# Attention steps of a fused decay-attention and two-MLP kernel: y, scores and decayed operands placed in three units instead of two

## Chip, cores and metric

One core of one Trainium2 chip. The metric is device time in microseconds (us), the median of the runs shown. Engines: TensorE (PE, with its weight loads as PEld), VectorE (DVE), ScalarE (ACT), GpSimd (POOL), SyncE (SP, which here only issues DMAs).

## What is computed

A decayed linear attention over r, k, v (4 x 8 heads x 768 tokens x 48), followed by two MLPs on 3072 tokens of width 384 with 2048 hidden columns. Cut to its core:

```python
for t in range(S):                       # attention, state [B, H, D, D]
    cur = einsum('bhd,bhe->bhde', u * k_t, v_t)
    y[:, :, t] = einsum('bhd,bhde->bhe', r_t, state + cur)
    state = w * state + einsum('bhd,bhe->bhde', k_t, v_t)
x = y.transpose(0, 2, 1, 3).reshape(B * S, H * D)
h = x @ w_in;  x = maximum(h, 0) ** 2 @ w_out          # layer 1
h = x @ w_in2; out = (h - tanh(h)) @ w_out2            # layer 2
```

## The kernel before

**Blocks and units.** The 3072 tokens are six blocks (`j`) of 512. A layer of a block is 16 units (`f`), one for each 128 hidden columns. A unit has `gemm1` (L579: 9 matmuls of 128x512 into `h`) and `gemm2` (L619 in layer 1, L729 in layer 2: 9 matmuls into the three banks `acc`). Each float32 operand is held as a high and a low part, so that a product is three matmuls of parts; `hi` and `lo` of the hidden values are `ghi` and `glo`. The loop over `units` runs all of layer 1 and then all of layer 2. In each turn it issues `gemm1` and the activation of a later unit (`front`, one unit ahead in most of block 0, two ahead after) and then `gemm2` of its own.

**Attention steps.** 24 steps of 128 tokens (two sub-steps of 64) make up the six blocks. Steps 0 to 3 are computed before the loop. Steps 4 to 23 are spread over the units of layer 1, four in each of blocks 0 to 4, where block j computes the steps of block j+1. A step i has these parts:

- `load` (L188 to L196): five DMAs on SP's queue for r/k (`rkt`), r (`rnt`), k (`kn`) and v (`vs`).
- `att_u`, `att_r`, `att_k`, `att_d` (L276 to L308) on POOL and the reduction `att_s` (`bt`, L293) on VectorE. They go through the list `nat_q`: `nat_push` puts six entries in, `nat_pop` issues two in each unit.
- `att_a` (L319, two of L322): k and r times the decay tables, on VectorE, into `rkt` and `ra`. `state_0` (L382 on ScalarE, L385 on VectorE): copies of the state into `vs`, and the decayed state.
- `att_b` (L351, 32 matmuls): scores `sc`. `att_v` (L362, 32 matmuls): state products `pv`.
- `att_m` (L372, two on VectorE): the masked scores into `ra`. `state_1` (L399, L385, L404 on VectorE, two L382 on ScalarE): the new state.
- `att_c` (L413, 32 matmuls): y from `ra` and `vs`. `att_e`: two copies on ScalarE (`ys`, `xt`, L430) and two subtractions on VectorE (L432). `pack` (L440): six DMAs.

Scores, state and y have one PSUM bank each (5, 6, 7). `vs` has three buffers, `ra`, `kn`, `rkt` and `rnt` have two.

**Weights of layer 1.** All 16 units' weights are converted while block 0 runs and stay on the chip. For unit f: `load_w` (L70, SP, three buffers `raw`), `conv0` (L84, ScalarE), `conv1` (L92 and L93, VectorE), `conv2` (L101, ScalarE: the high part), `conv3` (L107, the low part; on VectorE in the loop, on POOL before it). In turn f of block 0 the kernel issues `conv2` and `conv3` of unit f+2, `load_w` of f+5, `conv1` of f+3 and, at the end, `conv0` of f+4. `act1_low` (L608, VectorE) makes `glo` in blocks 0 and 5; in blocks 1 to 4 POOL does (L599). Layer 2's weights are converted in the same way from block 4 on: in its unit 11 the attention's memory is given back, the constants of layer 2 are set and five `load_w` are issued; `conv0(2, 0)` comes in unit 12.

**Order.** The schedule is manual: every engine and queue works through its instructions in the order in which the program issues them, and only waits between engines shift them. In a turn of block 0 the order before is: `glo` of the unit, conv2 and conv3, `load_w`, `front`, conv1, then the attention parts, `gemm2`, `att_m` and `state_1`, the two of `nat_pop`, conv0. In units 1, 4, 7, 10 (`visit`) the attention parts are `att_b(i+1)`, `att_v(i+1)`, `att_c(i)`, `att_e(i)`, `pack(i)`, `load(i+3)`; in units 0, 3, 6, 9 they are `att_a` and `state_0` of the step whose scores follow in the next unit.

Of the kernel before, what the change touches and what calls it, by code (L numbers as in the profile page):

```python
# [25 lines left out]
def decay_attention_moe_moe_kernel(  # L26
# [11 lines left out]
    NTAU, GP, _, NP, C = rk.shape  # L38
# [7 lines left out]
    NB = NT // TB  # L46
    TPB = TB // C
# [33 lines left out]
    def conv0(layer, f):  # L81
        if f < NF:
            lo, hi = words(layer, f)
            nc.scalar.activation(  # L84
                out=hi.bitcast(F32), in_=hi.bitcast(F32), func=AF.Prelu,
                scale=2.0 ** -112, alpha=2.0 ** 32,
            )
# [203 lines left out]
    def att_s(i):  # L291
        bt_t[i] = a2.tile([128, 2, NP], F32, tag="bt", name="bt")
        nc.vector.tensor_reduce(  # L293
            out=bt_t[i].rearrange("p c P -> p (c P)"), in_=rn_t[i].rearrange("p (x d) -> p x d", d=D),
            axis=mybir.AxisListType.X, op=ALU.add,
        )
# [445 lines left out]
        del acc[j]  # L742


    visit = {1: 0, 4: 1, 7: 2, 10: 3}
    units = [(1, j, f) for j in range(NB) for f in range(NF)]
    units += [(2, j, f) for j in range(NB) for f in range(NF)]

# [16 lines left out]
    with tc.manual_schedule():  # L765
        table_a()
        clear()
        for i in range(TPB):
            first(i)
            if i == 2:  # L770
                load_w(1, 0)
        for a in range(2):
            nc.scalar.dma_start(out=ub[half(a)], in_=u[1:2, a * GPS:(a + 1) * GPS].to_broadcast([64, GPS]))
        load_w(1, 1)
        load_w(1, 2)
        setup_pool()
        fill(WARM)
        V, G = nc.vector, nc.gpsimd

        def rs(i):  # L780
            if i != 3:
                lead_r(i, V)
            lead_s(i)

        def mb(i):
            for e in range(2):
                lead_m(2 * i + e)
                if i + 1 < TPB:
                    lead_b(2 * i + 2 + e)

        lead_z(0)
        lead_z(1)
        table_b()
        lead_a(0)
        lead_u(0, G)
        lead_zc(0)
        lead_b(0)
        lead_b(1)
        rs(0)
        lead_d(0)  # L800
        lead_zc(1)
        table_c()
        table_d()
        lead_u(1, G)
        lead_a(1)
        lead_k(0, G)
        fill(FILL[0])
        mb(0)
        lead_u(2, G)
        rs(1)  # L810
        lead_d(1)
        lead_k(1, G)
        lead_a(2)
        for i in range(TPB):
            lead_c(i)
            fill(FILL[1][i])
            if i + 2 < TPB:
                rs(i + 2)
            if i + 1 < TPB:
                mb(i + 1)  # L820
            if i < 2:
                load(i + 4)
            lead_e(i)
            if i + 2 < TPB:
                lead_zc(i + 2)
                lead_d(i + 2)
                lead_k(i + 2, G)
            if i + 3 <= TPB:
                (lead_u if i + 3 < TPB else att_u)(i + 3, G)
            if i + 3 < TPB:  # L830
                if i == 0:
                    lead_r(3, G)
                lead_a(i + 3, G)
            if i == 0:
                conv0(1, 0)
                conv1(1, 0)
                conv2(1, 0)
                conv3(1, 0, G)
            if i == 1:
                conv0(1, 1)  # L840
                att_r(4, G)
            if i == 2:
                conv1(1, 1)
            if i == 3:
                conv2(1, 1)
                conv3(1, 1, G)
        load_w(1, 3)
        conv0(1, 2)
        att_s(4)
        att_d(4, 0)  # L850
        att_d(4, 1)
        front(0)
        att_a(4)
        state_0(4)
        att_k(4, G)
        att_b(4)
        att_v(4)
        conv1(1, 2)
        att_m(4)
        state_1(4)  # L860
        nat_push(5)
        load_w(1, 4)
        load(6)
        conv2(1, 2)
        conv3(1, 2, G)
        load_w(1, 5)
        conv0(1, 3)
        nat_pop(3)
        front(1)
        nat_pop(3)  # L870

        nf = 2
        for n, (layer, j, f) in enumerate(units):
            if layer == 1:
                act1_low(j, f)
            if layer == 1 and j == 0 and f:
                conv2(1, f + 2)
                conv3(1, f + 2, V)
                if f + 5 < NF:
                    load_w(1, f + 5)  # L880
            if layer == 1 and j == NB - 1 and 0 < f < NF - 1:
                conv2(2, f - 1)
                conv3(2, f - 1, V)
            while nf < len(units) and nf <= n + look(n):
                front(nf)
                nf += 1
            att = layer == 1 and j + 1 < NB and f in visit
            if layer == 1 and j == 0:
                conv1(1, f + 3)
            if layer == 1 and j + 1 < NB and f - 2 in (-2, 1, 4, 7):  # L890
                i = TPB * (j + 1) + visit.get(f - 2, -1) + 2
                if i < NTAU:
                    att_a(i)
                    state_0(i)
            if att:
                i = TPB * (j + 1) + visit[f]
                if i + 1 < NTAU:
                    att_b(i + 1)
                    att_v(i + 1)
                att_c(i)  # L900
                att_e(i)
                pack(i)
                load(i + 3)
            if layer == 2 and j == 0 and f in (1, 2):
                conv2(2, NF - 3 + f)
                conv3(2, NF - 3 + f, G)
            if layer == 1:
                gemm2_1(j, f)
            else:
                gemm2_2(j, f)  # L910
            if att and i + 1 < NTAU:
                att_m(i + 1)
                state_1(i + 1)
                nat_push(i + 2)
            if layer == 1:
                nat_pop()
            if layer == 1 and j == 0:
                conv0(1, f + 4)
            if layer == 1 and j == NB - 2:
                if f == 11:  # L920
                    at_ctx.close()
                    open2()
                    for q in range(5):
                        load_w(2, q)
                if f == 12:
                    conv0(2, 0)
                if f == 14:
                    conv1(2, 0)
                    conv0(2, 1)
            if f == NF - 1:  # L930
                (evac1 if layer == 1 else evac2)(j)
            if layer == 1 and j == NB - 1:
                conv1(2, f + 1)
                conv0(2, f + 2)
                prep_x2(0, f)
            if layer == 2 and j + 1 < NB:
                prep_x2(j + 1, f)
# [72 lines left out]
```

## Time and profile before

| | |
|---|---|
| median of 3 runs | 943.94 us (943.58 to 943.96) |
| profiled execution | 943.92 us |
| its span, first to last instruction | 942.1 us |
| mean granted TensorE clock | 0.976 |
| busy: PE, DVE, ACT, POOL | 898.2, 650.8, 632.9, 251.1 us |

A profile is one execution. "Busy" is the time in which an engine had an instruction running. In rows of a timeline, the start and the length of a group of instructions come first, both in us; a bracket at the end is the idle time of that engine just before it and what ended it. "x9" is the number of instructions. The granted clock (PEclk) is 1.00 at 2.4 GHz and 0.50 at 1.2 GHz. Times in us from the start of the span.

### The profile page before, as it was taken

To read this page: it belongs to the slowest core of one execution; us is meant where nothing else is said; L and a number is where in the kernel's file an instruction comes from. 1 tells how busy PE (TensorE), PEld (TensorE's weight loads), DVE (VectorE), ACT (ScalarE), POOL (GpSimd) and SP (SyncE) were. 2 spreads that over 40 slices of the span, in tenths; PEclk is the share of its full clock that TensorE was granted. 3 is DMA by queue.
4 is the path that set the end of the run, shared out by engine and by line. 5 is a ranking of instruction groups with operands and counts; after the bars stand their busy time and mean duration, and the time that the engine had idled before them with its cause. 6 is when DMAs were issued, how large, how long until landed. Compare 5 with 4: busy or idle time off the path is not lost.

```text
span 942.1 us, 14863 instructions
## 1 busy us (share of the span) xinstructions
PE 898.2 (95%) x5688; PEld 739.4 (78%) x5688; DVE 650.8 (69%) x1016; ACT 632.9 (67%) x1121; POOL 251.1 (27%) x214
## 2 busy tenths in 40 slices
PE   6778889999999999999999999999999999999997
PEld 5656667888788788878888877888888888888885
DVE  8868886351424153133157789999999999999997
ACT  2535556444454545444478888898898988988985
POOL 4753332555365356444301011001001001000000
PEclk7978899999999999999999999999999999999999
DMA  8824442232132123120346210010010100100000
GB/s 241 236 85 151 151 152 67 62 90 59 49 84 77 57 56 93 49 84 9 130 167 213 98 57 12 1 56 12 1 57 13 56 12 1 56 12 0 34 1 34
DMA packets 32167, 67.72 MB, mean 72 GB/s; under 512 B 5600, under 2 KB 17888, under 8 KB 32096
## 3 DMA queue, kind: packets, MB, share of 16 engines
q1 hardware_dynamic: 31792, 66.48, 22.6%
q8 instruction: 45, 0.74, 0.3%
q10 hardware_dynamic: 304, 0.30, 0.1%
q14 instruction: 26, 0.21, 0.1%
HBM read 55.35 MB, written 9.44 MB: 69 GB/s over the span
## 4 chain that ended last, share of the span: by engine, by line
PE 80%; DVE 10%; ACT 4%; DMA 2%; POOL 2%; issue 1%; ACTq 0%; DVEq 0%; POOLq 0%
PE h L579 36%; PE o L729 19%; PE acc L619 17%; PE y L413 3%; PE sc L351 2%; PE pv L362 2%; DVE raw L93 1%; DVE ra L322 1%; DVE w L107 1%; DVE raw L92 1%; DMA x2d<-x2s 1%; DMA first_kv<-in_nat_dram 1%; DVE rkt L319 1%; DMA vtab<-in_w_dram 1%; DVE ra L372 1%
## 5 line engine op out<-in xcount | busy, mean ns | idle before, releaser
L579 PE MATMUL h<-xt,w 128*128 128x512 f32 x864 | 213.2, 392 | 0.0
L579 PE MATMUL h<-xs,w 128*128 128x512 f32 x864 | 211.5, 389 | 0.0
L579 PEld LDWEIGHTS h<-xt,w 128*128 128x128 f32 x864 | 163.2, 189 | 34.4
L579 PEld LDWEIGHTS h<-xs,w 128*128 128x128 f32 x864 | 162.2, 188 | 34.1
L619 PE MATMUL acc<-ghi,w 128*128 128x512 f32 x576 | 152.9, 396 | 3.5 <-ACT x2s L635 3.5
L729 PE MATMUL o<-ghi,w 128*128 128x512 f32 x576 | 148.9, 390 | 0.3 <-ACT ghi L700 0.3
L619 PEld LDWEIGHTS acc<-ghi,w 128*128 128x128 f32 x576 | 106.9, 189 | 28.0 <-ACT x2s L635 5.2
L599 POOL TENSOR_TENSOR glo<-g,ghi 128x512 fp32r<-128x512 f32 x64 | 84.0, 1313 | 164.3 <-PE acc L619 96.8
L593 ACT ACTIVATE g<-h 128x512 f32<-128x512 f32 x96 | 57.3, 597 | 104.3 <-PE h L579 104.1
L729 PEld LDWEIGHTS o<-ghi,w 128*128 128x128 f32 x576 | 107.7, 188 | 24.1 <-ACT ob L740 1.3
L432 DVE TENSOR_TENSOR ys<-y,ys 112x128 fp32r<-112x128 f32 x20 | 5.8, 292 | 149.9 <-ACT xt L430 149.9
L652 POOL TENSOR_TENSOR xs<-x2f,xs 128x512 fp32r<-128x512 f32 x18 | 24.4, 1354 | 316.7 <-DVE xs L651 316.7
L619 PE MATMUL acc<-glo,w 128*128 128x512 f32 x288 | 83.5, 391 | 3.8 <-DVE glo L608 3.7
L729 PE MATMUL o<-glo,w 128*128 128x512 f32 x288 | 84.2, 394 | 2.0 <-DVE glo L706 1.9
L676 ACT ACTIVATE th<-h 128x512 f32<-128x512 f32 x96 | 57.6, 600 | 41.9 <-DVE hy L675 41.9
L689 DVE SCALAR_TENSOR_TENSOR hy<-q,hy 128x512 f32<-128x512 f32 x96 | 78.4, 816 | 0.1
L675 DVE SCALAR_TENSOR_TENSOR hy<-h,y 128x512 f32<-128x512 f32 x96 | 66.1, 689 | 13.5 <-ACT y L673 13.3
L694 DVE COPY_PREDICATED hy<-mask,th 128x512 f32<-128x512 uint8 x96 | 70.9, 738 | 0.0
L679 DVE TENSOR_TENSOR th<-h,th 128x512 f32<-128x512 f32 x96 | 66.2, 689 | 5.9 <-ACT th L676 0.7
L677 ACT ACTIVATE q<-y,ba 128x512 f32<-128x512 f32 x96 | 68.6, 714 | 0.0
L680 ACT ACTIVATE q<-y,bb 128x512 f32<-128x512 f32 x96 | 68.5, 713 | 0.0
L683 ACT ACTIVATE mask<-y,bm 128x512 uint8<-128x512 f32 x96 | 68.3, 711 | 0.0
(105 smaller groups left out, 1255.3 us busy)
## 6 DMA issues: line engine op xcount, KB each, us to landing
raw<-in_w_dram SPq DMA_DIRECT2D x32, 768.0 KB, 4.7
rkt<-in_rk_dram SPq DMA_DIRECT2D x20, 448.0 KB, 4.2
x2d<-x2s SPq DMA_DIRECT2D x18, 256.0 KB, 2.3
x2f<-x2d SPq DMA_DIRECT2D x18, 256.0 KB, 3.2
out_dram<-ob SPq DMA_DIRECT2D x18, 256.0 KB, 2.2
rnt<-in_nat_dram SPq DMA_DIRECT2D x20, 192.0 KB, 4.1
kn<-in_nat_dram SPq DMA_DIRECT2D x20, 192.0 KB, 4.4
vs<-in_nat_dram SPq DMA_DIRECT2D x40, 96.0 KB, 4.0
```

Of the source, the lines that this page charges most:

```text
L579: nc.tensor.matmul(h, lhsT=w_in(layer, f, part, kk), rhs=x[:, xpart, kk, :], start=(n == 0), stop=(n == 3 * KK - 1),)
L599: nc.gpsimd.tensor_tensor(lo, g, hi.bitcast(F32), op=ALU.subtract)
L619: nc.tensor.matmul(acc[j][m], lhsT=w_out(1, f, part, m * 128, (m + 1) * 128), rhs=g, start=(f == 0 and n == 0), stop=(f == NF - 1 and n == 2),
L675: nc.vector.scalar_tensor_tensor(out=hy, in0=h, scalar=PK, in1=y, op0=ALU.mult, op1=ALU.mult)
L676: nc.scalar.activation(out=th, in_=h, func=AF.Tanh)
L677: nc.scalar.activation(out=q1, in_=y, func=AF.Square, bias=p2["ba"], scale=1.0)
L679: nc.vector.tensor_tensor(th, h, th, op=ALU.subtract)
L680: nc.scalar.activation(out=q2, in_=y, func=AF.Square, bias=p2["bb"], scale=1.0)
L683: nc.scalar.activation(out=mask, in_=y, func=AF.Sign, bias=p2["bm"], scale=1.0)
L689: nc.vector.scalar_tensor_tensor(out=hy, in0=q2, scalar=PD, in1=hy, op0=ALU.add, op1=ALU.mult)
L694: nc.vector.copy_predicated(hy, mask, th)
L729: nc.tensor.matmul(acc[j][m], lhsT=w_out(2, f, part, m * 128, (m + 1) * 128), rhs=g, start=(f == 0 and n == 0), stop=(f == NF - 1 and n == 2),
```

## The change

The units that hold `att_c`, `att_e` and `pack` move from 1, 4, 7, 10 to 2, 5, 8, 11. `att_b`, `att_v`, `load` (now of step i+2), `att_m` and `state_1` of the next step move out of that unit into the one behind it (3, 6, 9, 12, and the very first unit), and `att_a` and `state_0` of the step after that into the one behind that (4, 7, 10, 13, and the second unit). `nat_push` stays with `att_c`. Before the loop, `front(0)` and the conversion of unit 2 are issued ahead of step 4's parts, and scores, state and mask of step 4 and `load(6)` move into the loop.

```diff
-    visit = {1: 0, 4: 1, 7: 2, 10: 3}
+    visit = {2: 0, 5: 1, 8: 2, 11: 3}
...
         load_w(1, 3)
         conv0(1, 2)
+        front(0)
+        conv1(1, 2)
         att_s(4)
         att_d(4, 0)
         att_d(4, 1)
-        front(0)
+        conv2(1, 2)
+        conv3(1, 2, G)
         att_a(4)
         state_0(4)
         att_k(4, G)
-        att_b(4)
-        att_v(4)
-        conv1(1, 2)
-        att_m(4)
-        state_1(4)
-        nat_push(5)
         load_w(1, 4)
-        load(6)
-        conv2(1, 2)
-        conv3(1, 2, G)
         load_w(1, 5)
         conv0(1, 3)
-        nat_pop(3)
         front(1)
-        nat_pop(3)
+        nat_push(5)
+        nat_pop(2)
...
             att = layer == 1 and j + 1 < NB and f in visit
             if layer == 1 and j == 0:
                 conv1(1, f + 3)
-            if layer == 1 and j + 1 < NB and f - 2 in (-2, 1, 4, 7):
-                i = TPB * (j + 1) + visit.get(f - 2, -1) + 2
-                if i < NTAU:
-                    att_a(i)
-                    state_0(i)
             if att:
                 i = TPB * (j + 1) + visit[f]
-                if i + 1 < NTAU:
-                    att_b(i + 1)
-                    att_v(i + 1)
                 att_c(i)
                 att_e(i)
                 pack(i)
-                load(i + 3)
+            nxt = layer == 1 and j + 1 < NB and (f - 1 in visit or n == 0)
+            if nxt:
+                i = TPB * (j + 1) + visit.get(f - 1, -1) + 1
+                nxt = i < NTAU
+            if nxt:
+                att_b(i)
+                att_v(i)
+                load(i + 2)
+            if layer == 1 and j + 1 < NB and (f - 2 in visit or n == 1):
+                i2 = TPB * (j + 1) + visit.get(f - 2, -1) + 2
+                if i2 < NTAU:
+                    att_a(i2)
+                    state_0(i2)
...
-            if att and i + 1 < NTAU:
-                att_m(i + 1)
-                state_1(i + 1)
+            if nxt:
+                att_m(i)
+                state_1(i)
+            if att:
                 nat_push(i + 2)
```

## Rows read from the trace of the kernel before

**Rows 1.** The page, busy time, share of the span and instructions of each engine.

```profile
PE 898.2 (95%) x5688; PEld 739.4 (78%) x5688; DVE 650.8 (69%) x1016; ACT 632.9 (67%) x1121; POOL 251.1 (27%) x214
```

**Rows 2.** The page, busy tenths in 40 slices of 23.6 us.

```profile
PE   6778889999999999999999999999999999999997
...
DVE  8868886351424153133157789999999999999997
```

**Rows 3.** Stretches: length, then busy us of each engine, granted clock, DMA share, GB/s.

```profile
68.68:91.79 23.11, 18.47 (x151) 15.59 (x150) 18.68 (x24) 12.21 (x21) 7.20 (x5) 0.85 0.47 153
...
171.15:186.72 15.57, 15.57 (x151) 13.02 (x151) 6.97 (x12) 7.58 (x15) 8.98 (x9) 1.00 0.26 75
```

**Rows 4.** The chain of waits in block 0: start, length, what ran.

```profile
82.52 1.40 DVE ra L322
...
84.69 1.86 PE sc L351 x29
...
88.34 1.95 PE y L413 x32
...
91.00 0.29 DVE ys L432
```

**Rows 5.** Timeline of VectorE in block 0.

```profile
37.12 0.54 DVE L293 TENSOR_REDUCE bt<-rnt 128x8 f32<-128x384 f32 x1
...
52.74 0.55 DVE L293 TENSOR_REDUCE bt<-rnt 128x8 f32<-128x384 f32 x1 [4.88 <-POOL rnt L282]
...
67.89 0.29 DVE L432 TENSOR_TENSOR ys<-y,ys 112x128 fp32r<-112x128 f32 x1 [2.94 <-ACT xt L430]
...
72.88 0.96 DVE L107 TENSOR_TENSOR w<-raw,w 128x768 fp32r<-128x768 f32 x1 [1.11 <-ACT w L101]
...
76.31 1.79 DVE L107 TENSOR_TENSOR w<-raw,w 128x768 fp32r<-128x768 f32 x1
...
87.00 0.96 DVE L93 SCALAR_TENSOR_TENSOR raw<-raw 128x768 uint32<-128x768 uint32 x1
91.00 0.29 DVE L432 TENSOR_TENSOR ys<-y,ys 112x128 fp32r<-112x128 f32 x1 [3.04 <-ACT xt L430]
...
114.12 0.29 DVE L432 TENSOR_TENSOR ys<-y,ys 112x128 fp32r<-112x128 f32 x1 [3.04 <-ACT xt L430]
...
136.36 0.29 DVE L432 TENSOR_TENSOR ys<-y,ys 112x128 fp32r<-112x128 f32 x1 [2.14 <-ACT xt L430]
```

**Rows 6.** Timeline of PE in blocks 0 and 4.

```profile
54.40 0.96 PE L619 MATMUL acc<-glo,w 128*128 128x512 f32 x3 [2.74 <-DVE glo L608]
...
84.02 0.45 PE L351 MATMUL sc<-ra,rkt 48*64 48x64 f32 x2 [4.42 <-issue]
...
150.36 4.26 PE L579 MATMUL h<-xt,w 128*128 128x512 f32 x18
...
440.45 1.15 PE L413 MATMUL y<-ra,vs 128*64 128x64 f32 x32
```

**Rows 7.** Stretches of 1 us after two of PE's waits; the granted clock is third last.

```profile
84.00:85.00 1.00, 0.75 (x8) 0.58 (x10) 0.97 (x3) 0.51 (x1) 0.00 (x0) 0.50 0.00 0
...
54.00:55.00 1.00, 0.60 (x3) 0.51 (x4) 1.00 (x2) 0.00 (x0) 1.00 (x1) 1.00 0.07 31
```

**Rows 8.** Timeline of ScalarE in block 0.

```profile
37.73 0.90 ACT L84 ACTIVATE raw<-raw 128x768 f32<-128x768 f32 x1
...
70.42 0.74 ACT L382 ACTIVATE vs<-s 48x192 f32<-48x192 f32 x2 [2.57 <-DVE s L399]
71.17 0.91 ACT L84 ACTIVATE raw<-raw 128x768 f32<-128x768 f32 x1
71.98 0.87 ACT L101 ACTIVATE w<-raw 128x768 fp32r<-128x768 f32 x1
...
81.02 0.90 ACT L84 ACTIVATE raw<-raw 128x768 f32<-128x768 f32 x1 [2.31 <-DMA raw<-in_w_dram]
```

**Rows 9.** The page, DMA issues: KB of one, median us from issue to landing.

```profile
rnt<-in_nat_dram SPq DMA_DIRECT2D x20, 192.0 KB, 4.1
```

**Rows 10.** Timelines of VectorE and ScalarE in block 4.

```profile
443.13 1.50 DVE L372 COPY_PREDICATED ra<-low,sc 64x512 f32<-64x512 uint32 x2
...
444.89 0.74 ACT L382 ACTIVATE vs<-s 48x192 f32<-48x192 f32 x2 [2.59 <-DVE s L399]
```

**Rows 11.** Timelines of SP's queue and ScalarE in block 4, units 11 and 12.

```profile
462.16 2.72 SPq L70 DMA_DIRECT2D raw<-in_w_dram  x5
...
466.63 0.94 ACT L84 ACTIVATE raw<-raw 128x768 f32<-128x768 f32 x1 [1.05 <-DMA raw<-in_w_dram]
```

## The prediction, made before the change was run

> **What bounds the kernel now.** I read the engine totals first [rows 1], then the 40 slices [rows 2]. TensorE is busy 95% of the span, so the kernel looks bound by its matmuls; but in the slices the PE line holds 9s only from the eighth slice on, while in the first seven (0 to 165 us) it holds 6 to 8, and VectorE as much or little less beside it. Whatever the change gives must come from there: 44 us of the span (942.1 less 898.2) have no matmul, and most of them lie in that stage.
>
> Next the stretches [rows 3]. A round of three units in token block 0 takes 23.11 us; three units of block 1, with the same matmuls and an attention step, take 15.57 us with PE busy throughout. So block 0 isn't bound by TensorE. VectorE is busy 18.68 us of a round, since it converts the weights of layer 1 as well. That is not 23.11 either, so each round holds a wait.
>
> The chain of waits shows it [rows 4]. It runs through VectorE's `att_a` (ra L322), crosses to PE for scores, state and y (L351, L362, L413), to ScalarE for the copies of y, and comes back to VectorE at `ys` L432. VectorE's own view prices the excursion [rows 5]: its conversions end at 87.96 and it sits idle for 3.04 us until `ys`; in the other rounds for 2.94, 3.04 and 2.14 us. A second wait, 1.11 us, stands before one `w` L107 in each round. PE has the other side [rows 6]: it waits 4.42 us for `att_a`. In units 1, 4, 7, 10 PE does `att_b(i+1)`, `att_v(i+1)`, `att_c(i)` in that order: the y of step i, whose inputs are long ready, stands in PE's queue behind scores whose input VectorE has only just begun. Each engine waits for the other once a round. TensorE's clock adds to it [rows 7]: after that wait 0.50 is granted (1.2 of 2.4 GHz), so scores and y take 1.86 and 1.95 us [rows 4]; in block 4 y takes 1.15 [rows 6].
>
> **The change, part by part.** The instructions are the same; their order in five queues is not. What follows is their place in block 0.
>
> *y first, scores a unit later.* `att_c(i)` now follows only gemm1 of the next unit; its scores and state were made two units before. PE does it right after that gemm1, by my order some 5 us before VectorE gets to `ys`, which in VectorE's queue stands behind the `glo`, `w` and two `raw` of its unit. ScalarE's copies of y stand behind act1 of the next unit and are done before `ys` too. The four waits before `ys` go: 2.94 + 3.04 + 3.04 + 2.14 = **11.2 us off** [rows 5].
>
> *`att_a` two units ahead of `att_b`.* PE's 4.42 us before the scores go, but PE gains nothing by itself: gemm2 needs the `glo` of its unit, which VectorE makes at the unit's start. A round of VectorE without waits is 23.11 - 3.04 - 1.11 = 18.96 us, PE's is 15.57, so VectorE stays the bound and PE still waits some 3.5 us a round, now for `glo`.
>
> *The wait before `w` L107.* It is ScalarE's: after `s` it does two state copies, conv0 and conv2 [rows 8], while VectorE has three short items. In the new order the reduction `bt` (0.5 us) falls into that stretch, so of 1.11 us some 0.6 is left: 4 x 0.5 = **2 off**.
>
> *POOL.* Its five operations of a step still start when `bt` ends and run 7.2 us [rows 3] over the same VectorE items as now, where `w` takes 1.79 us beside POOL and 0.96 without [rows 5]. Nothing is lost; the 0.6 us left before `w` now falls inside POOL's work, so about 0.5 us of slowing a round goes: **2 off**, bounds 0 and 3.
>
> *Start.* Before the loop VectorE now does conv1 of unit 2 ahead of `att_s(4)`, and scores and state of step 4 move into unit 0. A wait of 4.88 us for POOL goes (POOL stood behind a conversion that ScalarE held up) [rows 5]. New are: conv1's wait for ScalarE's conv0, which ends at 38.63 [rows 8], where VectorE could begin `bt` at 37.12 [rows 5], 1.5 us; 0.6 before `w` in unit 1; and two `raw` operations beside POOL's conversion, about 0.9. **1.9 off**, bounds 0 and 4.
>
> *Clock.* PE's idle time will fall mostly in one piece, while VectorE does `raw`, `raw`, `att_a`, `dec`: by my order about 4 us in one round, and 1 us in the next if the clock fell and its matmuls were slower. A wait of 4.42 us cost the higher clock; after one of 2.74 us (before `glo`, unit 0) it was still 1.00 [rows 6, 7]. After a fall gemm1 and scores take twice as long and VectorE's `att_m` waits some 0.7 us for them. Two rounds of four: **1.4 on**, bounds 0 and 4.
>
> *DMAs.* `load` (five issues) moves from behind the six of `pack` to the next unit, behind `att_b` and `att_v`, and fetches step i+2, not i+3: two units instead of three from issue to `att_u`. Two units are 8 us or more; a transfer lands 4.1 us after its issue [rows 9]. `load_w` waits in SP's queue behind `pack` or `load` as it does now. Nothing on the path: 0.
>
> *Blocks 1 to 4, PE-bound.* Between the state matmuls and y of a step now lie only gemm2, gemm1, gemm2, gemm1. A gemm is half of 4.26 us [rows 6], so 8.5 us. In that time VectorE masks (from 443.13 on) and adds, and ScalarE copies (to 445.63) [rows 10]: 2.5 us. 0, and no gain either: PE waits for nothing there now.
>
> *Turn to layer 2.* The last y moves from unit 10 to 11 of block 4, and with it its six `pack` issues, ahead of the five `load_w` of layer 2. These leave one unit later than 462.16, some 4.3 us, and conv0 on ScalarE, which waits 1.05 us for the first now, waits 5.3 [rows 11]. Behind it stand act1 of unit 15 and of block 5's first unit. By my order they and the evacuation of `acc` end 0.2 to 1.5 us before PE wants them: **0.3 on**, bounds 0 and 2.
>
> The sum: -11.2 - 2 - 2 - 1.9 + 1.4 + 0.3 = -15.4 us. From gemm1 of unit 15 on (150.36 now [rows 6]) PE is continuous but for the waits of about 1 us at the blocks' ends, so the gain of the stage reaches the end whole. PE must be there too: from the last `glo` it waits for (unit 11) to that gemm1 it has a third of a gemm2, four gemms and two attention groups, 0.7 + 8.5 + 2.3 = 11.5 us, 3 more if the clock fell; VectorE takes about 12 to `w` of unit 15 (two thirds of a 19 us round). They come out together, so PE can cost or spare a microsecond or two. The profiled execution took 943.92 us (span 942.1 and 1.8 around it), the median is 943.94: the same to 0.02. 943.9 - 15.4 is 928.5; as the unit by unit order of VectorE alone came out nearer -16.5, I take **928.0 us**. Its own range: 934 with start, clock and turn at their worse bounds, 924.5 with the better ones.
>
> **Rivals.** (1) *The clock stays low.* PE in block 0 waits in more and smaller pieces than before. If 0.50 were granted throughout, a round's 15.57 us of matmuls would take about 30 us, longer than 23.11: PE would bound, and four rounds of 7 us more make 28, about 972. It decides where more than half of a round is at 0.50 (15.57 + 14.4 x share = 23.11 at 0.52). Against: a round with a 4.42 us hole in it has 0.85 [rows 3], and a 2.74 us hole left 1.00 [rows 7]. The Trainium skill ("TensorE: Matmul & The Clock Gate", section "A second HAM failure mode: psum-queue depth-cycling") says that frequent micro-idles between groups of matmuls make the clock oscillate; by that rule this case would come true, and no row here shows it for short holes. 5%.
>
> (2) *Weights late.* ScalarE already waits 2.31 us for `raw` in a round [rows 8]. If rounds shorter by 4 us moved that onto VectorE's path, 2 to 3 us of each round's gain would go: 8 to 12 back, 936 to 940. Against: conv1 comes a unit after conv0, and by my order each slice lands 4 us or more before VectorE wants it. 9%.
>
> (3) *The wait only moves*: VectorE waits for scores before `att_m` as long as for y now; 942 to 945. PE would have to reach `att_b` 3 us later than by the order above. 3%.
>
> (4) *Two units don't do in blocks 1 to 4*: 16 steps at 1 us each eat the gain. A margin of 6 us stands against it. 2%.
>
> **Numbers.** Forecast 81%. A measurement of this kernel tells about 0.2% (1.9 us) from no change. Faster by more: 0.91 (forecast, and rival 2 with its smaller gain); same 0.03; slower 0.06 (rival 1, and half of 4). The range is the forecast's own, 924 to 934.
>
> **What would show it.** Right: in block 0 no wait before `ys`; rounds of 19 to 20 us with VectorE busy in over 95% of them; gemm1 of unit 15 at 132 to 136 us; block 1 rounds still 15.57 us; PE's largest waits before `glo` (L619). Wrong: rounds over 21 us, a wait of VectorE before `att_m`, a granted clock under 0.7 over a round, a hole in PE near 470 us.

## The result, and the profile after

The changed kernel takes **927.83 us** (median of four runs, 927.79 to 927.89) against 943.95 for the kernel before beside it: a ratio of 0.9829, 95% interval 0.9812 to 0.9846, that is 16.1 us or 1.7% faster. The forecast was 928.0 with a range of 924 to 934. The profiled execution took 927.85 us with a span of 926.0, against 943.92 and 942.1, so the two traces show the whole difference. The time came out as forecast, but two terms of the sum did not, and that they cancelled was luck; the trace shows where.

The page after, with the lines that answer to [rows 1] and [rows 2]:

```profile
PE 896.6 (97%) x5688; PEld 731.8 (79%) x5688; DVE 638.8 (69%) x1016; ACT 631.8 (68%) x1121; POOL 255.1 (28%) x214
...
PE   6799989999999999999999999999999999999997
...
DVE  8899971332242233123167799999999999999996
...
PEclk7989999999999999999999999999999999999999
```

The same instructions, and PE is busy for 1.6 us less; what shrank is its idle time, from 44 us to 29. PE's 9s now begin in the third slice (with one 8 in the sixth) instead of the seventh (the prediction counted the eighth: before, PE is below 9 in six slices, up to 141 us, not in seven), and VectorE's heavy stretch ends in the sixth instead of the seventh.

VectorE's timeline after, one round of block 0 (start, length, what ran, the idle time before it), answers to [rows 4, 5]:

```profile
71.42 0.54 DVE L293 TENSOR_REDUCE bt<-rnt 128x8 f32<-128x384 f32 x1
...
73.23 1.08 DVE L107 TENSOR_TENSOR w<-raw,w 128x768 fp32r<-128x768 f32 x1 [0.66 <-ACT w L101]
74.23 1.42 DVE L92 TENSOR_SCALAR raw<-raw 128x768 uint32<-128x768 uint32 x1
75.68 0.96 DVE L93 SCALAR_TENSOR_TENSOR raw<-raw 128x768 uint32<-128x768 uint32 x1
...
77.16 2.11 DVE L322 TENSOR_TENSOR ra<-rkt,tr 48x512 f32<-48x512 f32 x2
79.28 1.06 DVE L385 TENSOR_TENSOR dec<-st,wdec 112x192 f32<-112x192 f32 x1
...
82.32 1.66 DVE L93 SCALAR_TENSOR_TENSOR raw<-raw 128x768 uint32<-128x768 uint32 x1
83.89 0.28 DVE L432 TENSOR_TENSOR ys<-y,ys 112x128 fp32r<-112x128 f32 x1
...
91.84 1.07 DVE L107 TENSOR_TENSOR w<-raw,w 128x768 fp32r<-128x768 f32 x1 [0.67 <-ACT w L101]
```

No bracket stands before `ys` any more: the waits of 2.14 to 3.04 us are gone. The one before `w` is 0.66 instead of 1.11. A round, from one such `w` to the next, takes 91.84 - 73.23 = 18.61 us, and the next two (to 109.98 and 127.93) 18.14 and 17.95, where the round of [rows 3] took 23.11.

The stretches (length, busy us of each engine, granted clock, DMA share, GB/s): block 0 from the loop's start to gemm1 of unit 15, the first round, a stretch that begins 1 us after one of PE's waits, the end of the last round, and a round of block 1.

```profile
36.40:131.34 94.94, 83.99 (x713) 67.25 (x711) 89.56 (x118) 61.59 (x105) 46.44 (x30) 0.91 0.55 168
73.23:91.84 18.61, 16.76 (x148) 13.23 (x147) 17.69 (x24) 12.67 (x21) 8.53 (x6) 0.91 0.63 197
...
82.00:83.00 1.00, 1.00 (x4) 0.81 (x3) 0.97 (x2) 0.33 (x1) 1.00 (x1) 0.50 0.25 49
...
118.00:128.00 10.00, 9.47 (x89) 7.67 (x90) 9.80 (x18) 4.67 (x8) 0.42 (x1) 0.83 0.11 21
...
153.03:168.81 15.78, 15.78 (x152) 12.94 (x151) 6.15 (x12) 7.46 (x15) 7.50 (x7) 1.00 0.25 74
```

VectorE is busy 95% of that first round of block 0. In block 1 the round grew from 15.57 us to 15.78, with PE busy for all of it: that is a loss, and it was not forecast. PE's timeline, answering to [rows 6], shows both ends:

```profile
81.00 1.09 PE L619 MATMUL acc<-glo,w 128*128 128x512 f32 x3 [1.85 <-DVE glo L608]
...
118.53 1.07 PE L619 MATMUL acc<-glo,w 128*128 128x512 f32 x3 [3.49 <-DVE glo L608]
119.39 3.74 PE L579 MATMUL h<-xt,w 128*128 128x512 f32 x9
...
131.34 4.24 PE L579 MATMUL h<-xt,w 128*128 128x512 f32 x18
...
153.03 1.15 PE L413 MATMUL y<-ra,vs 128*64 128x64 f32 x32
...
158.42 1.15 PE L351 MATMUL sc<-ra,rkt 48*64 48x64 f32 x32
159.40 1.09 PE L362 MATMUL pv<-vs,kn 64*64 64x48 f32 x32
```

gemm1 of unit 15 moved from 150.36 to 131.34, 19.0 us earlier. The matmuls after it gave 2.9 of those back. The landmark is the first copy of `acc` that closes a block, on VectorE, in the timelines of before and then of after; the first and the last of five:

```profile
160.10 0.69 DVE L633 COPY x2s<-acc 128x512 f32<-128x512 f32 x1 [4.83 <-PE acc L619]
...
477.19 0.69 DVE L633 COPY x2s<-acc 128x512 f32<-128x512 f32 x1 [8.63 <-PE acc L619]
```

```profile
141.06 0.69 DVE L633 COPY x2s<-acc 128x512 f32<-128x512 f32 x1 [4.83 <-PE acc L619]
...
461.02 0.69 DVE L633 COPY x2s<-acc 128x512 f32<-128x512 f32 x1 [5.30 <-PE acc L619]
```

From first to last it is 317.1 us before and 320.0 after. So the result is -19.0 in block 0, +2.9 in blocks 1 to 4, and nothing after that.

### The profile page after: what moved, and what is told of

Same layout as the page of the kernel before. It is cut to its first block, busy times and chain, and to the rows that moved or that the text cites. A ratio compares the mean times of both kernels' runs of the same rounds, so it can differ in the third digit from the quotient of the medians.

```text
span 926.0 us, 14869 instructions
## 1 busy us (share of the span) xinstructions
PE 896.6 (97%) x5688; PEld 731.8 (79%) x5688; DVE 638.8 (69%) x1016; ACT 631.8 (68%) x1121; POOL 255.1 (28%) x214
## 4 chain that ended last, share of the span: by engine, by line
PE 83%; DVE 8%; ACT 4%; DMA 3%; issue 1%; SPq 0%; POOL 0%; ACTq 0%; DVEq 0%; POOLq 0%
PE h L579 37%; PE o L729 20%; PE acc L619 18%; PE y L413 2%; PE sc L351 2%; PE pv L362 2%; DVE ra L322 1%; DMA first_kv<-in_nat_dram 1%; DMA x2d<-x2s 1%; DVE w L107 1%; DMA raw<-in_w_dram 1%; DVE raw L92 1%; DVE raw L93 1%; DVE ra L372 1%; ACT x2s L635 1%
## 5 line engine op out<-in xcount | busy, mean ns | idle before, releaser
L619 PE MATMUL acc<-ghi,w 128*128 128x512 f32 x576 | 156.0, 402 | 3.3 <-ACT x2s L635 3.3
L619 PEld LDWEIGHTS acc<-glo,w 128*128 128x128 f32 x288 | 54.2, 189 | 20.2 <-DVE glo L608 8.7
```

Source lines behind the costliest of these rows:

```text
L619: nc.tensor.matmul(acc[j][m], lhsT=w_out(1, f, part, m * 128, (m + 1) * 128), rhs=g, start=(f == 0 and n == 0), stop=(f == NF - 1 and n == 2),
```

## The experiments

In each, `before` and `changed` name the kernel that the edit starts from. Blocks 1 to 4 were compared by the four distances between those copies of `acc`: 79.80, 79.91, 79.70 and 77.68 us before, 80.62, 80.53, 80.53 and 78.28 in the changed kernel.

**y ahead of scores, nothing else** (on `before`):

```diff
-                if i + 1 < NTAU:
-                    att_b(i + 1)
-                    att_v(i + 1)
                 att_c(i)
                 att_e(i)
                 pack(i)
+                if i + 1 < NTAU:
+                    att_b(i + 1)
+                    att_v(i + 1)
```

> The kernel before with one edit: in units 1, 4, 7, 10 y of step i is issued ahead of scores and state of step i+1; all stays in one unit, and att_a stays one unit ahead of the scores. Theory A (the price in block 0 was VectorE's wait for a y that stood behind scores; breaking that order is enough): the waits before ys go, 943.9 - 11.2 = 932.7 us, 930 to 934, gemm1 of unit 15 at 138 to 140 us, no wait of VectorE before att_m, and blocks 1 to 4 as long as before (79.8 us each), as y, scores and state stay side by side. Theory B (the distance in units is what counts; without it PE waits 4 us for att_a as before and VectorE's wait moves to att_m): 940 to 944.

Measured: 934.99 us (932.92 to 935.53), ratio 0.9896 (0.9882 to 0.9911); blocks 1 to 4 79.80, 79.71, 79.68 and 77.66, as before. Its VectorE and PE timelines:

```profile
85.22 0.28 DVE L432 TENSOR_TENSOR ys<-y,ys 112x128 fp32r<-112x128 f32 x1
...
90.21 0.96 DVE L107 TENSOR_TENSOR w<-raw,w 128x768 fp32r<-128x768 f32 x1 [1.11 <-ACT w L101]
```

```profile
81.36 0.30 PE L351 MATMUL sc<-ra,rkt 48*64 48x64 f32 x2 [3.51 <-issue]
```

PE still waits 3.51 us for `att_a`, and VectorE no longer waits before `ys`: its rounds fall to 20.1 us on average, 23.11 less the 3.04 of the wait. Of the two waits, only the one on the bounding engine cost time in the rounds. The second wait, 1.11 before `w`, stays. The time is 1 us above the range that was expected: at the end of unit 15's `w` VectorE is 10.4 us earlier than before (140.44 against 150.83), but gemm1 of that unit starts only 8.4 us earlier (141.97), as PE came out of the stage last here.

**`att_a` two units ahead of the scores, y still behind them** (on `before`):

```diff
-            if layer == 1 and j + 1 < NB and f - 2 in (-2, 1, 4, 7):
-                i = TPB * (j + 1) + visit.get(f - 2, -1) + 2
+            if layer == 1 and j + 1 < NB and (f - 1 in visit or n == 0):
+                i = TPB * (j + 1) + visit.get(f - 1, -1) + 2
```

> The kernel before with one edit: att_a and state_0 of a step come two units ahead of its scores (units 2, 5, 8, 11), not one; scores, state, y stay in one unit in the old order. For the first such step (5) nothing changes, its att_a was in the first unit already. Theory A: y still stands behind the scores, but these find their input ready, so three of the four waits before ys go (3.04 + 3.04 + 2.14 us) and the first (2.94) stays: 935 to 936 us, blocks 1 to 4 as before. Theory C (the order y before scores is needed, an early att_a alone is not enough): 940 to 944.

Measured: 938.39 us (937.30 to 939.12), ratio 0.9939 (0.9922 to 0.9956). Its VectorE timeline:

```profile
68.07 0.29 DVE L432 TENSOR_TENSOR ys<-y,ys 112x128 fp32r<-112x128 f32 x1 [2.95 <-ACT xt L430]
...
87.95 0.28 DVE L432 TENSOR_TENSOR ys<-y,ys 112x128 fp32r<-112x128 f32 x1
```

Only the first wait is left, since step 5's `att_a` keeps its old place there, and the rounds take 19.84 us. The time is 2.4 us above the 936 expected: the three waits that went were 8.2 us, but gemm1 of unit 15 moved by 6.6 (to 143.75), and what took the rest is not settled. Either of the two moves cures the cycle, in which y stood in PE's queue behind scores that VectorE had not fed yet. They are not worth twice as much together, as the next run shows.

**The changed kernel with scores and state joined to y again in all blocks** (on `changed`; the offset `f - 1` of scores becomes `f`, that of `att_a` `f - 1`):

```diff
-            nxt = layer == 1 and j + 1 < NB and (f - 1 in visit or n == 0)
+            nxt = layer == 1 and j + 1 < NB and (f in visit or n == 0)
...
-            if layer == 1 and j + 1 < NB and (f - 2 in visit or n == 1):
-                i2 = TPB * (j + 1) + visit.get(f - 2, -1) + 2
+            if layer == 1 and j + 1 < NB and (f - 1 in visit or n == 1):
+                i2 = TPB * (j + 1) + visit.get(f - 1, -1) + 2
...
```

> The changed kernel with one thing undone in all blocks: scores and state of step i+1 stand directly behind y of step i in units 2, 5, 8, 11, att_a one unit behind that (two units ahead of its scores); the new part ahead of the loop is kept. y goes first and att_a is early, so VectorE has no wait before ys. Theory D (what the split into three units adds in block 0 is that POOL's five operations meet other instructions of VectorE, and bt lies in the wait before w: rounds of 18.2 us after against 20.2 in e1 and 19.8 in e2): block 0 is about 6 us longer than after, blocks 1 to 4 2.9 us shorter: 929 to 932. Rival (the split itself adds nothing; after beats e1 and e2 by its start and by PE's freedom alone): 924 to 926.

Measured: 930.89 us (929.73 to 931.96), ratio 0.9862 (0.9847 to 0.9877), rounds of 19.87 us, blocks 1 to 4 79.80, 79.72, 79.70 and 77.68. So with both moves and the new start the split into three units is worth another 1.3 to 1.9 us a round in block 0, and costs 2.9 us in blocks 1 to 4.

**The old start** (on `changed`, with the part ahead of the loop as before):

```diff
-        front(0)
-        conv1(1, 2)
         att_s(4)
...
+        front(0)
         att_a(4)
         state_0(4)
         att_k(4, G)
+        att_b(4)
+        att_v(4)
+        conv1(1, 2)
+        att_m(4)
+        state_1(4)
+        nat_push(5)
...
-            nxt = layer == 1 and j + 1 < NB and (f - 1 in visit or n == 0)
+            nxt = layer == 1 and j + 1 < NB and f - 1 in visit
```

> The changed kernel with the part ahead of the loop as before (step 4's scores, mask and state, load(6) and the conversion of unit 2 in the old order), the loop as changed. Theory A: the second unit's att_a then ends some 2.6 us later, as in the traces (64.95 against 62.34), and VectorE bounds the stage to its end, where PE has about 1.6 us of lag behind it: 927.8 plus 1 to 2.6, 929 to 930.5. Rival: PE is the bound by the end of block 0 in any case and the start was worth nothing: 927.5 to 928.3.

Measured: 929.73 us (929.34 to 930.98), ratio 0.9847 (0.9832 to 0.9862); gemm1 of unit 15 at 132.52 and the 4.9 us wait before `bt` back. VectorE ends unit 15's `w` at 132.55 where the changed kernel ends it at 129.74, so the new start is worth 2.8 us to VectorE; gemm1 keeps 1.2 of that and the medians 1.9. That is the size expected, but the two intervals overlap, and block 0 scatters by more (below).

**Split in block 0 only, joined in blocks 1 to 4** (on `changed`):

```diff
-            nxt = layer == 1 and j + 1 < NB and (f - 1 in visit or n == 0)
+            nxt = layer == 1 and j + 1 < NB and ((f if j else f - 1) in visit or n == 0)
...
-                i = TPB * (j + 1) + visit.get(f - 1, -1) + 1
+                i = TPB * (j + 1) + visit.get(f if j else f - 1, -1) + 1
...
-            if layer == 1 and j + 1 < NB and (f - 2 in visit or n == 1):
+            if layer == 1 and j + 1 < NB and (f - (1 if j else 2) in visit or n == 1):
...
-                nat_push(i + 2)
+                nat_push(TPB * (j + 1) + visit[f] + 2)
```

> The changed kernel in block 0; in blocks 1 to 4 scores and state of step i+1 stand directly behind y of step i in units 2, 5, 8, 11, and att_a one unit later than that. Theory A (after, blocks 1 to 4 take 0.7 us more each, because two groups of small matmuls between gemms cost PE 0.2 us more than one group, 15 or 16 times): 927.8 - 2.9 = 924.9, 924.5 to 925.4, a step's round in block 1 back at 15.57 us from 15.77. Rival (the 0.7 us come from other queues, POOL or the evacuation at a block's end): 927.3 to 928.3.

Measured: 924.78 us (923.15 to 926.63), ratio 0.9793 (0.9777 to 0.9809); blocks 1 to 4 79.81, 79.72, 79.71 and 77.66. PE's timeline, one round of block 1:

```profile
154.74 1.15 PE L413 MATMUL y<-ra,vs 128*64 128x64 f32 x32
155.82 1.15 PE L351 MATMUL sc<-ra,rkt 48*64 48x64 f32 x32
156.80 1.09 PE L362 MATMUL pv<-vs,kn 64*64 64x48 f32 x32
...
170.31 1.15 PE L413 MATMUL y<-ra,vs 128*64 128x64 f32 x32
```

15.57 us again: the 2.9 us come from giving scores and state a group of their own, and not from y going first or from an early `att_a`, which stay as in the changed kernel.

**Three groups a step** (on `changed`; in blocks 1 to 4 `att_v`, `load` and `state_1` one unit later than the scores, and `nat_push` one unit later than it was):

```diff
                 att_b(i)
-                att_v(i)
-                load(i + 2)
+                if j == 0:
+                    att_v(i)
+                    load(i + 2)
+            late = layer == 1 and 0 < j and j + 1 < NB and f - 2 in visit
+            if late:
+                iv = TPB * (j + 1) + visit[f - 2] + 1
+                late = iv < NTAU
+            if late:
+                att_v(iv)
+                load(iv + 2)
...
```

> The changed kernel with the state matmuls, state_1, load and nat_push of blocks 1 to 4 one unit later than the scores: three groups of small matmuls a step between gemms in place of two; block 0 as changed. Theory A (each further group costs PE 0.2 us): 15 more groups, 927.8 + 3 = 930.8, 930 to 932, blocks 1 to 3 81.3 us each, a step's round 15.98 us. Rival (the 0.7 us a block of after come from elsewhere): 927.3 to 928.5.

Measured: 932.22 us (930.95 to 933.27), ratio 0.9875 (0.9859 to 0.9892), blocks 82.15, 82.03, 82.00 and 79.39. A round of block 1 lies between these lines of PE's timeline:

```profile
168.40 1.15 PE L413 MATMUL y<-ra,vs 128*64 128x64 f32 x32
...
184.54 1.15 PE L413 MATMUL y<-ra,vs 128*64 128x64 f32 x32
```

The direction is as expected, the size is not: the round went to 16.14 us, so the third group cost 0.36 us where the second cost 0.21.

**Two groups, cut elsewhere** (on `changed`, in blocks 1 to 4), to tell a price for each group from a price for each change of shape:

```diff
                 pack(i)
+                if j and i + 1 < NTAU:
+                    att_v(i + 1)
...
                 att_b(i)
-                att_v(i)
+                if j == 0:
+                    att_v(i)
```

> The changed kernel, but in blocks 1 to 4 the state matmuls (64x64 operands) move out of the group with the scores and stand directly behind y: still two groups of small matmuls a step, now {y, state} and {scores} instead of {y} and {scores, state}. TensorE's rounds of three units have been 15.57 us (one group), 15.78 (two groups: y | scores, state) and 16.14 us (three groups). Counting groups, the third cost 0.36 where the second cost 0.21, which does not fit one price for a group. Theory 'a price for each change of the operands' shape': between gemms (128x128), y (128x64) and scores and state (both of tiles up to 64x64) the shape changes 3, 4 and 6 times in those rounds, 0.18 to 0.21 us for each change; scores ran 0.98 us from start to start before state, 1.08 before a gemm. Here it changes 5 times, so the round should be 15.88 to 15.97 us, blocks 1 to 3 (80.5 to 80.6 us from evacuation to evacuation in the changed kernel) 81.0 to 81.4, the whole some 1.5 to 3 us longer: 929 to 931. The Trainium skill ("TensorEngine Tiling (Array Packing)", section "Key Properties") says that changing the tiling mode, and not only the tile, drains TensorE; it gives no price, and this order would show whether that bears on it. Rival, 'a price for each group between gemms': two groups as in the changed kernel, so 15.78 us and 80.5 to 80.6 again, 927 to 928.5. A second rival, that the third group of the earlier run cost more because VectorE or ScalarE delayed it there, expects 15.78 too.

Measured: 930.23 us (927.76 to 931.22), ratio 0.9854 (0.9837 to 0.9870), blocks 81.30, 81.19, 81.15 and 78.76. PE's timeline:

```profile
166.48 1.15 PE L413 MATMUL y<-ra,vs 128*64 128x64 f32 x32
167.56 1.13 PE L362 MATMUL pv<-vs,kn 64*64 64x48 f32 x32
...
172.95 1.15 PE L351 MATMUL sc<-ra,rkt 48*64 48x64 f32 x32
174.03 1.66 PE L619 MATMUL acc<-ghi,w 128*128 128x512 f32 x6
...
182.42 1.15 PE L413 MATMUL y<-ra,vs 128*64 128x64 f32 x32
```

The round is 15.94 us. With 3, 4, 5 and 6 changes of shape the rounds take 15.57, 15.78, 15.94 and 16.14 us: 0.16 to 0.21 for each, whatever the number of groups. Scores followed by state matmuls take 0.98 us from start to start, scores followed by a gemm 1.08. The Trainium skill ("TensorEngine Tiling (Array Packing)", section "Key Properties") says that changing the tiling mode drains TensorE; these four rounds agree with it, at 0.16 to 0.21 us for a change of operand shape. What inside PE takes the time, no row shows.

**Less work for POOL**, on the kernel with y first and on the changed one. From step 6 on POOL's products of u, r and k (`att_u`, `att_r`, `att_k`) are left out, and only `att_d` stays:

```diff
-                lambda: att_u(i, G), lambda: att_r(i, G), lambda: att_s(i),
-                lambda: att_k(i, G), lambda: att_d(i, 0), lambda: att_d(i, 1),
+                (lambda: att_u(i, G)) if i < 6 else none, (lambda: att_r(i, G)) if i < 6 else none, lambda: att_s(i),
+                (lambda: att_k(i, G)) if i < 6 else none, lambda: att_d(i, 0), lambda: att_d(i, 1),
```

> Kernel e1 (y first in one unit) without att_u, att_r and att_k on POOL from step 6 on; these products are left out. POOL keeps att_d. Theory D (VectorE is slowed by POOL's operations beside it, and the split into three units moves them to where they slow it less): a round of block 0 falls from 20.2 to about 17.8 us, 935 to 925-928, and the distance to e8 shrinks from 7 us to 0 to 3. Rival (waits and PE make the distance): 930 to 934, and 5 us or more to e8.

> The changed kernel without att_u, att_r and att_k on POOL from step 6 on; these products are left out. Theory D: VectorE is slowed less by them already, so a round falls only from 18.2 to 17 to 17.5 us, and PE soon bounds: 924.5 to 926.5. Rival: the same 4 us or more as in e7, 923 or less.

Measured: 924.26 us (two runs, ratio 0.9792, 0.9773 to 0.9812) and 919.25 (two runs, 0.9739, 0.9720 to 0.9759). By the ratios, 9.8 and 8.5 us go with these products, and VectorE's items (`w`, L92, L93, L319, L322, `dec`, `glo`) show where: in a round of block 0 they had run 4.0 and 2.2 to 3.2 us longer than alone, and now run 1.2 to 1.8 and 1.0 us longer. So POOL's slowing of VectorE is real. But both runs came out below what was expected, the second by 5 us, and the two kernels did not come together; 5.0 us are left between them. At the first copy of `acc` they are 7.8 us apart (140.79 and 133.00). Of these, 3.0 are there before the rounds, from the new start (VectorE is done with unit 1 at 63.35 and 60.36), and blocks 1 to 4, where the changed kernel is the slower one, give 3.1 back. The rest is in the rounds, and the reason stands in the VectorE timelines, first with y first, then the changed kernel:

```profile
70.61 0.54 DVE L293 TENSOR_REDUCE bt<-rnt 128x8 f32<-128x384 f32 x1
71.08 0.68 DVE L609 TENSOR_TENSOR glo<-g,ghi 128x512 fp32r<-128x512 f32 x1
71.70 1.80 DVE L107 TENSOR_TENSOR w<-raw,w 128x768 fp32r<-128x768 f32 x1
```

```profile
71.62 1.07 DVE L107 TENSOR_TENSOR w<-raw,w 128x768 fp32r<-128x768 f32 x1 [0.67 <-ACT w L101]
```

In the first, `att_d` on POOL runs beside `w`, which takes 1.80 instead of 0.95. In the second `bt` stands just ahead of the wait for ScalarE, so `att_d` begins inside it and `w` takes 1.07. That is 0.7 us a round, and the wait itself is 0.67 instead of 1.12: 1.2 us a round, some 4.6 if all four rounds were like this one. The expectation had all of the split's gain in the slowing by the other products, and this was wrong.

**conv2 a unit earlier, to take away the last 0.67 us** (on the kernel joined in blocks 1 to 4):

```diff
-                conv2(1, f + 2)
                 conv3(1, f + 2, V)
...
+            if layer == 1 and j == 0:
+                conv2(1, f + 3)
             if nxt:
                 att_m(i)
```

> The changed kernel once more, beside the two others on the same chip: 0.983 of the kernel before, gemm1 of unit 15 at 131 to 133 us, blocks 1 to 3 80.5 us each.

> Kernel e4 (the changed kernel in block 0, y with scores and state in one unit in blocks 1 to 4) on the same chip as r1. Theory A: 2.9 us less than r1. Rival (its 924.8 was the chip's): the same as r1 within 1 us.

> Kernel e4 with ScalarE's conv2 of block 0 issued one unit earlier, ahead of the state copies of state_1 (conv2 of unit f+3 late in turn f in place of f+2 at its start). It takes away the 0.67 us that VectorE still waits before w L107 in each round. Theory D: POOL's att_d now fills part of that wait, so without it att_d slows w by up to 0.7 us again and the gain is small: 0 to 2 us less than r2. Rival (a wait of 0.67 us is worth its length four times and no more slowing follows): 2.5 us less or more.

Measured on one chip: the changed kernel 927.48 (925.84 to 929.31; ratio 0.9825, 0.9807 to 0.9844; gemm1 of unit 15 at 129.24, earlier than expected), joined in blocks 1 to 4 925.79 (923.82 to 926.43; 0.9800, 0.9784 to 0.9816), with conv2 earlier 924.10 (922.14 to 926.97; 0.9791, 0.9766 to 0.9817). The wait before `w` is gone in the last, but `att_d` no longer falls into it: L93 takes 1.63 us and L319 1.54 beside POOL, where they take 0.96 and 0.68 alone. The gain of 1.7 is inside the spread. The joined kernel beats the changed one by 1.7 in the medians where the blocks of the two traces differ by 2.9; the intervals overlap, so by time alone that is not settled.

What these runs scatter by can be seen in the traces. Six traces have one and the same order in block 0 and differ in the granted clock at its end. Stretches 118 to 128 us of three of them, namely of the run with state behind y, of the three groups, and of the second joined one (the changed kernel's stands above):

```profile
118.00:128.00 10.00, 9.51 (x97) 7.53 (x95) 9.80 (x16) 5.32 (x9) 4.39 (x4) 1.00 0.21 64
```

```profile
118.00:128.00 10.00, 10.00 (x92) 7.90 (x92) 9.80 (x17) 5.05 (x8) 2.41 (x2) 0.83 0.16 42
```

```profile
118.00:128.00 10.00, 9.03 (x82) 7.14 (x83) 8.77 (x15) 3.09 (x6) 0.09 (x1) 0.66 0.13 35
```

At 1.00 the first copy of `acc` comes at 138.54 and (the changed kernel again) 138.96 us, at 0.83 at 140.24 and 141.06, at 0.66 at 142.66 and 142.75. VectorE's rounds are alike to 0.5 us until 110 in all six. In the two at 1.00, PE's last long wait for `glo`, which ended between 116 and 120, was 1.12 and 2.54 us; in those at 0.66 it was 3.48 and 3.50, and only there VectorE then waited for PE before `att_m` (1.09 and 1.14 us). At 0.83 it was 2.67 and 3.49, so the length of the wait alone does not sort them. An earlier wait shows this better; it is 2.66 us long both with state behind y and in the first joined trace:

```profile
82.27 1.65 PE L619 MATMUL acc<-glo,w 128*128 128x512 f32 x3 [2.66 <-DVE glo L608]
```

```profile
82.16 0.97 PE L619 MATMUL acc<-glo,w 128*128 128x512 f32 x3 [2.66 <-DVE glo L608]
```

From 83 to 84 us the granted clock is 0.50 in the one and 1.00 in the other. VectorE ends `w` of unit 15 between 129.66 and 131.35 in the six, and gemm1 of that unit starts between 128.81 and 133.03. So block 0 varies by 4 us between executions of one order, most of it on PE's side, and the second joined trace stands at its long end, the changed kernel's beside it at its short end.

## Why the prediction was right, point by point

**The cycle between y and scores** (-11.2): right in place and size. All waits before `ys` are gone, and each of the two single moves removes them (the early `att_a` all but the first, whose `att_a` it does not move).

**The wait before `w`** (-2): right. 1.11 became 0.66, as `bt` moved into it, and in the last round it is gone; after the start, 2.4 us less in block 0.

**The start** (-1.9): -2.6 in the trace. At 62.34, where `glo` of unit 2 begins, VectorE has done the items that it had done at 64.95 before, where its wait for the first `ys` began.

**POOL** (-2, bounds 0 and 3): this step failed, at -4.8. From there to the end of unit 15's `w` VectorE took 85.88 us before and takes 67.40 now. Of the difference of 18.5, 11.2 and 2.45 are waits, and 4.8 are work that ran faster (busy 68.87 and 64.06 us). I had said that POOL's operations run their 7.2 us "over the same VectorE items as now". They do not. POOL waits for the new `rnt` in the middle of its sequence (start, length, idle time before; POOL's timeline after):

```profile
72.14 3.09 POOL L303 TENSOR_TENSOR ra<-ident,bt 64x512 f32<-64x512 f32 x2 [11.33 <-DVE bt L293]
77.47 1.24 POOL L277 TENSOR_TENSOR rnt<-rnt,ub 128x384 f32<-128x384 f32 x1 [2.25 <-DMA rnt<-in_nat_dram]
...
98.19 2.13 POOL L277 TENSOR_TENSOR rnt<-rnt,ub 128x384 f32<-128x384 f32 x1 [4.37 <-DMA rnt<-in_nat_dram]
```

So part of its work moves to where VectorE reads PSUM or does items that POOL holds up less. In [rows 5]'s round `w`, L92, L93, L319, L322, `dec` and `glo` together run some 4.0 us longer than alone; in the three rounds after the like sums are 3.1, 2.2 and 3.2, and the lowest is that of the round with the wait of 4.37 us. In the kernel joined in all blocks they are 3.9, 3.6 and 3.8, so it is the split that lessens the slowing.

**DMAs** (0): the cost was right, the reason was not. I had the transfer land 4.1 us after its issue; in the loop, the one issued at 89.78 kept POOL waiting until 98.19. No VectorE item waited for it. That the round with this delay is the one with the least slowing (2.2 us) was luck.

**Clock** (+1.4, bounds 0 and 4): near in size, by another way. I had VectorE's `att_m` waiting for PE in two rounds. In the profiled execution it waits nowhere in block 0, but after PE's wait of 3.49 us at 118.53 the clock fell, gemm1 behind it took 3.74 us instead of 2.20, and PE came out of the stage last: VectorE's part ended 21.1 us earlier, gemm1 of unit 15 only 19.0. Gemm1 of unit 15 varies by 4.2 us over the six traces, about as wide as the bounds, so that the time came within 0.2 us of the forecast was luck. "They come out together, so PE can cost or spare a microsecond or two" was the sentence that mattered.

**Blocks 1 to 4** (0): this step failed, at +2.9. I looked only at whether PE would wait for another engine, and it does not. I did not ask what one group of small matmuls more does on PE itself: 0.21 us in each of 15 steps, shown by joining, by splitting further and by cutting elsewhere. The rows to see it were there: in a round of block 1 [rows 3] PE was busy throughout, so any matmul that takes longer counts in full. That "the gain of the stage reaches the end whole" was wrong by the same 2.9 us.

**Turn to layer 2** (+0.3): ScalarE's conv0 waits 4.38 us at 453.79 where 5.3 was forecast, and PE has no hole there. 0.

With the measured terms: -11.2 - 2.4 - 2.6 - 4.8 + 2.1 (PE last) = -18.9 to gemm1 of unit 15, and + 2.9 = -16.0; the trace has -16.1. The forecast of -16 was the sum of a gain of the stage that was 3 us too small and a cost of the later blocks that was left out.

**Signs.** No wait before `ys`, VectorE busy in 93 to 99% of a round, no wait before `att_m` in the profiled execution and PE's largest waits before `glo` came as forecast. The rounds were shorter than the 19 to 20 us, gemm1 of unit 15 came 0.7 us ahead of the 132 to 136, and block 1's round was not 15.57.

**Rivals.** None came true. The clock that stays low (972): it is 0.91 over the stage, with one fall at the start, for scores of step 4, and two of some 4 us each after waits of 1.85 and 3.49 us. PE's largest waits after (us in total, times, longest):

```profile
PE acc L619 <- DVE glo L608: 6.6, 4, 3.5
PE sc L351 <- DVE ra L322: 5.3, 2, 2.9
```

The Trainium skill ("TensorE: Matmul & The Clock Gate", section "A second HAM failure mode: psum-queue depth-cycling") tells of a kernel in which frequent micro-idles made the clock oscillate, which is not a clock that stays low. In this trace, with six waits in 95 us, it fell three times and stood at 1.00 in between.

The other rivals. Weights late: no wait of VectorE for `raw`'s DMA in the loop. Through ScalarE one round had a little of it: conv0 waited 1.42 us for `raw` until 101.14, conv2 ran behind it, and VectorE's `w` at 102.92 waited 0.35 us for that. The wait moving to `att_m`: only in the two traces at 0.66, with 1.1 us. Two units too few in blocks 1 to 4: PE is busy throughout the round of block 1 shown above.

## What to carry to other kernels

When two engines wait for each other once a round, look in the queue of each for an item whose inputs are ready and which stands behind one that is not; moving it in front is worth at most the wait on the bounding engine (11.2 us here; 9.8 came through when it was moved alone), and nothing for the other engine's wait. Spreading work over more places is good where a slower engine bounds, and has a price where the matmul engine does, so choose the order for each stage: split in block 0 and joined after it gave 0.979 to 0.980 of the time before, against 0.983 (the intervals overlap; that blocks 1 to 4 are 2.9 us shorter is seen in the traces). Two terms that cancel look like a confirmed sum, so check each term at its own landmark in the trace.

## What was not expected of the hardware

- Each change of the matmuls' operand shape cost PE 0.16 to 0.21 us (rounds of 15.57, 15.78, 15.94 and 16.14 us for 3 to 6 changes).
- The length of a single wait does not say whether the higher clock is lost: 0.50 was granted after one of 1.85 us (at 81.00, after), and 1.00 was kept after one of 2.74 [rows 6, 7]. One of 2.66 us, in the same place of the same order, cost it in one trace and not in another (82.27 and 82.16, above).
- Beside POOL, VectorE's conversions often take 0.7 to 0.9 us longer each (L92 1.42 for 0.55, L93 1.66 for 0.96). It can also be POOL's operation that runs longer: beside L285 at 80.20, which took 2.95 us (1.32 at 116.33), `w` took its 0.95. But `ys` and `xt`, which read PSUM, keep their 0.28 and 0.54 us at 101.06 beside a product on POOL. The Trainium skill ("SBUF — State Buffer", section "SBUF: two separate sides") says that the two engines share one pair of ports, that "the other fully blocks"; it names VectorE operations with two SBUF inputs or in a two-port mode. The rows agree for the two-input ones; L92, with one input, is held up as long, and no row shows its mode.
- Open: why one wait costs the clock and another of the same length does not, whether POOL's slowing can go without leaving its products out (this was not tried), and how far below 924 us the version split in block 0 alone would come if PE's last wait there stayed short.
